# Attention and two gated layers on one core: buffers as fixed tiles, maxima on 64 rows, reciprocals by a DRAM row, another order

## The chip, the cores and the metric

The kernel runs on one core of a Trainium2 chip. The metric is the device time of one execution, in microseconds (us). Engines are named as the profile names them: PE (TensorE, matmuls), PEld (its loads of weights, which overlap it), DVE (VectorE), ACT (ScalarE), POOL (GpSimd), SP (SyncE, which here only issues DMAs).

## What is computed

Attention for 4 batches of 8 heads, 576 positions of 64 numbers each, with a mask of blocks of 64; its result, 4 x 576 x 512, goes through a gated layer with a convolution, and that one's result through a second layer, gated along the positions. Cut to what matters, the reference is:

```python
def _attn_ref(q, k, v):                      # 4, 8, 576, 64
    scores = scale * np.matmul(q, k.transpose(0, 1, 3, 2))
    scores = np.where(block_i >= block_j, scores, -1e9)
    scores = scores - np.max(scores, axis=-1, keepdims=True)
    attn = np.exp(scores)
    attn = attn / (np.sum(attn, axis=-1, keepdims=True) + 1e-09)
    return np.matmul(attn, v)

def _moe_ref(x, w_in, conv_w, w_out):        # 512 -> 1024 -> 512
    h = np.maximum(x @ w_in, 0.0)
    conv_out = sum(conv_w[k] * shift(h, k - 1) for k in range(3))
    return (h * sigmoid(conv_out)) @ w_out

def _moe2_ref(x, w_in, w_spatial, b_spatial, w_out):
    h = np.maximum(x @ w_in, 0.0)
    u, v = h[..., :512], h[..., 512:]
    v_n = (v - mean(v)) / np.sqrt(var(v) + 1e-06)
    v_s = np.einsum('ts,bsd->btd', w_spatial, v_n) + b_spatial[None, :, None]
    return (u * v_s) @ w_out
```

## The kernel before

**Numbers in two parts.** TensorE multiplies values that are rounded to a shorter format in one pass, full float32 in four. To keep accuracy, most operands are held as a rounded value and a low part (`_h`, `_l`), and a product is three products: high by high, low by high, high by low. Making the two parts (a rounding copy and a subtraction, `minus`, `sub` L331) is work of ACT, POOL and DVE.

**Pairs.** Attention works on 16 pairs of heads, counted here from 0; four pairs make a batch. One pair passes through these steps:

- `prep_pair` (L461 to L508) loads q and k of a pair (`raw`, two heads on 128 partitions) and rounds them into `kp` and `qbd`. `qbd` is block-diagonal: nine blocks of 128 x 128, in which head 0's 64 queries stand on partitions and columns 0 to 63, head 1's on 64 to 127, and the rest is zero. Pairs 0 to 5 (`PF32` = 6) multiply their scores in float32 from `raw`; later ones also make low parts `kl`.
- `max_step` (L521) finds the maximum of each query over the keys it may see. Ten products with the 128 rows of `qbd`: for block 0 to 7 over 64, 128, ... 512 keys, for the last block two of 288. VectorE reduces each with its own TENSOR_REDUCE (L544; L537 for the last block in one). `max_tr` (L557) transposes the 128 x 9 maxima on TensorE (L563), copies them to `mt`, and a DMA for each head (L576) writes them as a row behind the queries, `mq`.
- `score`, `unit` (L604 to L664): products of keys and queries of the two heads abreast, each on 64 of the 128 rows (L620 in float32, L628 in parts), and one that adds mask and maximum (`mk`, `mq`, L632). ScalarE takes the exponentials (L641).
- `av` (L666): the attention values (L325), and with them the sums: for pairs 0 to 6 (`PONES` = 7) all as products with ones; for the others `add_up` (L695) adds the exponentials on DVE or POOL first.
- `v_out`, `s_out`, `norm_a`, `norm_b` (L713 to L782): values to `xpair`, sums to `srow`. A DMA (L742) packs the sums into `rc`, 36 x 32; DVE takes the reciprocal (L746); it is split into `rh` and `rl`, two DMAs (L756) write both as rows of `r4`, and TensorE spreads them over the partitions with a selector matrix `sel` (float32 rounded, 4 products with sums on PE, else 2; L761). DVE multiplies `xpair` by this from PSUM (L772); POOL rounds the result to `x` (L328), DVE or POOL makes its low part (L331).

**Dense layers.** `in1` (L788) makes one chunk of the hidden layer, 12 products of 290 columns; ACT, DVE (L814, two taps), ACT, DVE (L819) and POOL (L328) turn it into `g`. `out1` (L833) multiplies `g` by `w1o`, 24 products of 288 columns a chunk, in two parts. The weights come as 64-bit numbers in 512 KB pieces and are put together by `split64` (L402) and `words_to_f32` (L386): ACT, three on DVE (L394, L396, L398), a rounding on ACT and a subtraction. What follows attention (the second layer: `vtile`, `ustep`, `sstep`, `ostep`) works on one batch at a time.

**What sets the order.** Nothing in the program runs in a loop of its own: an `Order` object plays the kernel through in advance, with a cost for each step, and so fixes the sequence of instructions on every engine. Each step is a generator that takes a place in a ring of buffers, waits for marks, and queues work for an engine. TensorE's next step is chosen by `pick_at` from five streams: maxima (`xstream`, released by `next_x` with `XE` and `XK`), scores, values, `norm_b`, and the dense layers (`mstream`); `AHEAD` says how far each batch's dense layers may run ahead of attention. A change between products on 64 rows and on 128 rows has a cost there (`tile`). All loads are issued by SP in one sequence; the costs of a DMA are in `dma`. Buffers are rotating pools (`tag`, `bufs`): the next allocation takes the buffer that is the next in turn.

```python
MSTEPS = [[(0, 0, 0, 0, 64), (0, 64, 1, 0, 128), (0, 192, 2, 0, 192), (1, 0, 3, 0, 256)],
          [(0, 0, 4, 0, 320), (1, 0, 5, 0, 384)], [(0, 0, 6, 0, 448), (1, 0, 7, 0, 512)],
          [(0, 0, 8, 0, HT), (1, 0, 8, HT, HT)]]
```

Of the kernel before, what the change touches and what calls it, by code (L numbers as in the profile page):

```python
# [16 lines left out]
NP = H // 2  # L17
# [12 lines left out]
AHEAD = (0.47, 0.62, 0.22, 0.75)  # L30
PREP_AT = 8
PREP_DT = 2.5
PREP_DT2 = 2.5
PREP_AT2 = 36
# [3 lines left out]
PF32 = 6  # L38
X1KEEP = (0, 1)
PONES = 7  # L40
KL_POOL = 0xbe22
QL_POOL = 0xaa37
SGN_POOL = 0x1
M_ACT = 0xd8c6
Q_DVE = 0x0
PTWO = 5
P_KL = 2
NPR = 0
SPLIT = 2
# [40 lines left out]
class Order:  # L90
# [9 lines left out]
    def __init__(self, rings):  # L100
# [18 lines left out]
        self.times = {r: [-9.0] * n for r, n in rings.items()}  # L119

# [8 lines left out]
    def advance(self, gen, group):  # L129
        while True:  # L130
            try:
                it = next(gen)
            except StopIteration:
                self.live[group] -= 1
                return
            kind = it[0]
            if kind == "mark":
                self.mark(it[1])
            elif kind == "free":
                self.release(it[1], it[2] if len(it) > 2 else 1)  # L140
# [83 lines left out]
    def pe(self):  # L224
# [5 lines left out]
        for r, n in step["rings"]:  # L230
            self.grab(r, n)
# [3 lines left out]
        after = step["fn"]()  # L235
# [48 lines left out]
def attn_moe_moe2_kernel(  # L284
# [19 lines left out]
        "raw": NRAW, "mq": NQ, "kpq": NKP, "v": 2, "e0": NE[0], "e1": NE[1], "es": NES, "late": NRAW - 1, "xp": 2, "sr": 1, "r4": 1,  # L304
# [150 lines left out]
    def prep_pair(p, t):  # L455
# [35 lines left out]
        if p < PF32:  # L491
            return
# [972 lines left out]
```

## Time and profile before

| | |
|---|---|
| median of 3 runs | 604.42 us (603.97 to 608.26) |
| profiled execution | 608.3 us, span from first to last instruction 606.5 us |
| PE busy | 586.5 us (97%) |
| PEld busy | 526.9 us (87%) |
| DVE busy | 453.2 us (75%) |
| ACT busy | 258.6 us (43%) |
| POOL busy | 187.4 us (31%) |

The table by stretch in the rows below has one line for each piece of the span: from and to, its length, then for PE, PEld, DVE, ACT and POOL the busy us with the number of instructions, the clock granted to TensorE (1.00 is full), the busy share of the DMA engines and their GB/s. A line of a timeline gives start and length in us, the engine, the line of the program, output and inputs, the shape, and how often in a row; in brackets is how long it waited and for whom. Matmuls overlap, so a printed length is longer than the distance to the next start; prices of products are distances between starts. A line by form gives count, busy us and mean ns of one, and the idle time of the engine just before.

### The profile page before, as it was taken

To read this page: it belongs to the slowest core of one execution; us is meant where nothing else is said; L and a number is where in the kernel's file an instruction comes from. 1 tells how busy PE (TensorE), PEld (TensorE's weight loads), DVE (VectorE), ACT (ScalarE), POOL (GpSimd) and SP (SyncE) were. 2 spreads that over 40 slices of the span, in tenths; PEclk is the share of its full clock that TensorE was granted. 3 is DMA by queue.
4 is the path that set the end of the run, shared out by engine and by line. 5 is a ranking of instruction groups with operands and counts; after the bars stand their busy time and mean duration, and the time that the engine had idled before them with its cause. 6 is when DMAs were issued, how large, how long until landed. Compare 5 with 4: busy or idle time off the path is not lost.

```text
span 606.5 us, 12028 instructions
## 1 busy us (share of the span) xinstructions
PE 586.5 (97%) x4654; PEld 526.9 (87%) x4654; DVE 453.2 (75%) x964; ACT 258.6 (43%) x528; POOL 187.4 (31%) x237
## 2 busy tenths in 40 slices
PE   7989999999999999999999999999999999999997
PEld 5656679798888888989988999888989999998997
DVE  6889999886786985786938398977894676368257
ACT  4666645635436733526624375545342023013101
POOL 7323213533444353344503144442221112022021
PEclk9899999999999999999999999999999999999999
DMA  7555530214014014021010555335603300610012
GB/s 246 166 173 172 197 105 31 83 41 141 23 61 121 24 41 144 21 65 39 21 60 2 161 179 180 108 108 163 227 0 112 123 21 2 195 40 2 13 48 78
DMA packets 41927, 56.65 MB, mean 93 GB/s; under 512 B 9381, under 2 KB 34725, under 8 KB 41870
## 3 DMA queue, kind: packets, MB, share of 16 engines
q1 hardware_dynamic: 41380, 55.72, 28.7%
q8 instruction: 36, 0.59, 0.4%
q0 software_dynamic: 400, 0.16, 0.1%
q14 instruction: 21, 0.17, 0.1%
q10 hardware_dynamic: 90, 0.01, 0.0%
HBM read 41.42 MB, written 14.16 MB: 92 GB/s over the span
## 4 chain that ended last, share of the span: by engine, by line
PE 62%; DVE 23%; DMA 5%; POOL 3%; issue 2%; ACT 2%; SPq 1%; DVEq 0%; POOLq 0%; ACTq 0%
PE mo L317 38%; PE st L317 13%; PE st L325 4%; DVE cc L814 4%; PE st L628 4%; DVE mx L544 3%; DMA w_raw<-in_w2i_dram 2%; DVE w_f L398 2%; DVE w_raw L396 2%; DMA w_raw<-in_w1i_dram 2%; PE st L632 2%; PE st L620 2%; DVE cc L819 1%; DVE w_raw L394 1%; DVE g L331 1%
## 5 line engine op out<-in xcount | busy, mean ns | idle before, releaser
L317 PE MATMUL mo<-g,w1o_h 128*128 128x288 f32 x496 | 105.3, 298 | 1.2 <-DVE y L852 1.2
L317 PE MATMUL mo<-x,w1i_h 128*128 128x290 f32 x488 | 105.3, 301 | 0.7 <-ACT h L807 0.6
L317 PEld LDWEIGHTS mo<-g,w1o_h 128*128 128x128 f32 x496 | 81.5, 189 | 3.2 <-DVE y L852 1.6
L317 PEld LDWEIGHTS mo<-x,w1i_h 128*128 128x128 f32 x488 | 80.7, 189 | 3.3 <-ACT h L807 1.6
L814 DVE SCALAR_TENSOR_TENSOR cc<-h,cwt,cc 128x288 f32<-128x288 f32 x128 | 72.9, 583 | 10.2 <-ACT cc L811 9.6
L328 POOL TENSOR_SCALAR g<-cc 128x288 fp32r<-128x288 f32 x64 | 39.8, 624 | 113.4 <-DVE cc L819 108.2
L317 PE MATMUL mo<-g,w1o_l 128*128 128x288 f32 x248 | 73.2, 295 | 0.0
L317 PE MATMUL mo<-x,w1i_l 128*128 128x290 f32 x244 | 72.4, 297 | 0.0
L641 ACT ACTIVATE e<-st 128x640 f32<-128x640 f32 (+1 forms) x64 | 52.3, 837 | 29.7 <-PE st L632 29.0
L328 POOL TENSOR_SCALAR gt<-ga 128x288 fp32r<-128x288 f32 x40 | 19.8, 496 | 113.9 <-DVE ga L1160 74.1
L317 PE MATMUL mo<-x,w2i_h 128*128 128x288 f32 x256 | 52.2, 296 | 1.5 <-ACT u L1135 1.5
L544 DVE TENSOR_REDUCE mx<-st 128x1 f32<-128x320 f32 (+7 forms) x98 | 43.9, 481 | 5.6 <-PE st L317 5.3
L317 PEld LDWEIGHTS mo<-g,w1o_l 128*128 128x128 f32 x248 | 46.6, 188 | 0.2
L325 PE MATMUL st<-e,v 128*64 128x448 f32 (+4 forms) x384 | 46.7, 392 | 0.0
L317 PEld LDWEIGHTS mo<-x,w1i_l 128*128 128x128 f32 x244 | 46.1, 189 | 0.1
L325 PEld LDWEIGHTS st<-e,v 128*64 128x64 f32 x384 | 25.0, 137 | 23.4 <-issue 16.5
L317 PEld LDWEIGHTS mo<-x,w2i_h 128*128 128x128 f32 x256 | 41.4, 188 | 2.3 <-ACT u L1135 2.0
L317 PE MATMUL mo<-ws_h,vnh 128*128 128x288 f32 x135 | 39.3, 295 | 1.1 <-issue 1.1
L632 PE MATMUL st<-mq,mk 64*128 64x320 f32 (+1 forms) x192 | 37.7, 385 | 1.9 <-DMA mq<-mt 1.9
L317 PE MATMUL st<-w2i_h,x 128*128 128x512 f32 x128 | 39.5, 390 | 0.0
L331 DVE TENSOR_TENSOR gt<-ga,gt 128x288 fp32r<-128x288 f32 x56 | 25.5, 476 | 17.5 <-POOL gt L328 17.5
L811 ACT ACTIVATE cc<-h,cwt 128x288 f32<-128x288 f32 x64 | 34.1, 538 | 10.2 <-POOL g L335 6.0
(171 smaller groups left out, 1427.3 us busy)
## 6 DMA issues: line engine op xcount, KB each, us to landing
x2d<-y SPq DMA_DIRECT2D x32, 288.0 KB
x<-x2d SPq DMA_DIRECT2D x16, 576.0 KB
raw<-in_kq_dram SPq DMA_DIRECT2D x15, 576.0 KB
v<-in_vt_dram SPq DMA_DIRECT2D x16, 320.0 KB
out_dram<-o SPq DMA_DIRECT2D x32, 144.0 KB
w_raw<-in_w1i_dram SPq DMA_DIRECT2D x8, 512.0 KB
w_raw<-in_w1o_dram SPq DMA_DIRECT2D x8, 512.0 KB
w_raw<-in_w2i_dram SPq DMA_DIRECT2D x8, 512.0 KB
```

Of the source, the lines that this page charges most:

```text
L317: nc.tensor.matmul(o, w, x, start=start, stop=stop)
L325: nc.tensor.matmul(o[row:row + m], w, x, start=start, stop=stop)
L328: nc.gpsimd.tensor_scalar(o, i, 1.0, 0.0, ALU.mult, ALU.add)
L331: nc.vector.tensor_tensor(o, a, b, ALU.subtract)
L396: yield ("DVE", t_dve(n), lambda: nc.vector.scalar_tensor_tensor(r[:, :, 1], r[:, :, 0], 29, r[:, :, 1], ALU.logical_shift_right, ALU.bitw ...
L398: yield ("DVE", t_dve(n), lambda: nc.vector.scalar_tensor_tensor(f.bitcast(U32), f.bitcast(U32), 3, r[:, :, 1], ALU.logical_shift_left, AL ...
L544: yield ("DVE", t_dve(n), lambda: nc.vector.tensor_reduce(mx[:, c:c + 1], st[bk][:, o:o + n], AX.X, ALU.max), 0, 0)
L628: nc.tensor.matmul(st[:, e, o:o + nq], keys(kx, slice(64 * e, 64 * e + 64)), qx[e], start=j == 0, stop=False)
L632: nc.tensor.matmul(st[:, e, o:o + nq], keys(mk, r), q[r, q0:q0 + nq], start=False, stop=True)
L641: yield ("ACT", t_act(2 * n), lambda: nc.scalar.activation(ex[:, :, e0:e0 + n], st[:, :, 0:n], ACTF.Exp, scale=0.125), 0, 0)
L811: yield ("ACT", t_act(HT, False, 1), lambda: nc.scalar.activation(cc, h[:, o:o + HT], ACTF.Copy, scale=cwt[:, c, 1:2]), 0, P_G)
L814: yield ("DVE", t_dve(HT, ptr=1), lambda: nc.vector.scalar_tensor_tensor(cc, h[:, o + e:o + e + HT], cwt[:, c, j:j + 1], cc, ALU.mult, ALU ...
```

## The change

**Fixed tiles.** `Order` gets `slots`: `grab` returns the buffers themselves, in the order in which they came free, and `release` gives them back. Instead of pools that rotate there are fixed tiles, and whichever comes free first is the next.

**Maxima on 64 rows.** `qbd` goes. The rounded queries `qp` have the form of `kp`, two heads on 128 partitions, and only the last block stands block-diagonally in `qlast`. For the first 512 queries, `tile_max` multiplies 128 queries of one head by their keys on 64 rows, both heads one after the other into the two banks of a buffer: 128, 256, 384 and 512 columns. Since of 128 queries the upper 64 see 64 keys more, VectorE reduces in two instructions (all 128 partitions without the last 64 keys, and the upper 64 partitions over these), and `max_up` combines. `last_max` has the two products of 288 columns. These products count as `tile` steps now, as the scores do.

**Reciprocals by DRAM.** `rh`, `rl`, `r4`, `sel`, the selector products and the step `norm_b` go. The reciprocals `rc` are written to a row in DRAM, `rd`, and two DMAs read each head's row into 64 partitions of `rb` (`broadcast_to`). DVE multiplies `xpair` by `rb`, in one piece for pairs without sums on PE, and in three for the others.

**Numbers of the order.** Most of the planner's numbers and of the masks that say which engine does which copy change. Pairs with float32 scores are now 0, 1, 2, 4, 6, 7 and 9 (`F32_PAIRS`). A DMA's cost in the plan is changed (`RATE`, `HEAD`, `SLACK`).

```diff
-AHEAD = (0.47, 0.62, 0.22, 0.75)
-PREP_AT = 8
-PREP_DT = 2.5
-PREP_DT2 = 2.5
-PREP_AT2 = 36
+AHEAD = (0.05, 2.01, -0.09, 0.71)
+PREP_AT = 5.0
+PREP_DT = 1.4
+PREP_DT2 = 4.05
+PREP_AT2 = 45.0
-PF32 = 6
+F32_PAIRS = 0x2d7
-MARGIN = 0.4
+MARGIN = 0
-ADD_DVE = 0xffca
+ADD_DVE = 0x3674
-XE = (0.5, 1.75)
-XMO = 7
+XE = (0.95, 13.95)
+XMO = 11
...
     def grab(self, ring, n):
         self.free[ring] -= n
         del self.times[ring][:n]
+        got = self.slots[ring][:n]
+        del self.slots[ring][:n]
+        return got
...
-    yield ("DMA", size / 360e3 + 0.01, None, 0, 0)
-    yield ("sleep", DMA_LAG)
+    yield ("DMA", size / RATE + 0.01, None, 0, 0)
+    yield ("sleep", DMA_LAG + (SLACK if size > 65536 else 0.0))
...
+    QTILES = [[(0, 0), (1, 128)], [(2, 0)], [(3, 0)]]
+    def tile_max(p, j, i):
+        def fn(got):
+            kp, qp, _ = KPQ[p]
+            mx, up = maxima(p)
+            st = got["st"][0]
+            for c, o in QTILES[i]:
+                n = 128 * c + 128
+                for e in range(2):
+                    r = slice(64 * e, 64 * e + 64)
+                    nc.tensor.matmul(st[:, e, o:o + n], qp[r, 128 * c:128 * c + 128], kp[r, 0:n], start=True, stop=True)
...
+                for c, o in QTILES[i]:
+                    yield red(mx[:, c:8:4], st[:, :, o:o + 128 * c + 64])
+                if i == 0:
+                    yield red(up[64:128].rearrange("p (e c) -> p e c", e=2)[:, :, 0:2],
+                              st.rearrange("p e (i x) -> p e i x", x=256)[64:128, :, :, 64:128])
+                else:
+                    c = i + 1
+                    yield red(up[64:128, c:8:4], st[64:128, :, 128 * c + 64:128 * c + 128])
...
+    def last_max(p, j, ring):
...
+            for i in range(2):
+                mm(st[i][:, 0:HT], ql8, kp[:, HT * i:HT * i + HT], True, True)
...
+    def max_up(p):
+        for j in range(4):
+            yield ("wait", ("mx", p, j))
+        mx, up = MX[p]
+        yield ("DVE", 0.08, lambda: nc.vector.tensor_tensor(mx[64:128, 0:8], mx[64:128, 0:8], up[64:128], ALU.max), 0, 0, True)
...
     def norm_a(p, sr):
...
         yield ("DVE", 0.26, lambda: nc.vector.reciprocal(rc, rc), 0, NPR)
-        if (M_ACT >> p) & 1:
-            yield ("ACT", 0.2, lambda: nc.scalar.activation(rh, rc, ACTF.Copy), 0, NPR)
-        else:
-            yield ("DVE", 0.12, lambda: nc.vector.tensor_copy(rh, rc), 0, NPR, True)
-        yield ("DVE", 0.13, lambda: sub(rl, rc, raw(rh)), 0, NPR, True)
-        yield ("take", "r4")
-        def rows():
-            for t, x in enumerate((rh, rl)):
-                nc.sync.dma_start(out=raw(r4[2 * t:2 * t + 2, :]), in_=raw(x))
-        yield from dma(9216, rows, 0, 1.35)
+        yield from dma(4608, lambda: nc.sync.dma_start(out=rd[p], in_=rc), 0, 0.66)
         yield ("free", "rc")
+        yield ("take", "rb")
+        rb = att.tile([128, S], F32, name="rb", tag="rb", bufs=1)
+        def spread():
+            for e in range(2):
+                nc.sync.dma_start(out=rb[64 * e:64 * e + 64], in_=rd[p][e:e + 1].broadcast_to([64, S]))
+        yield from dma(294912, spread, 0, 0.9)
+        yield ("wait", ("vo", p))
+        cols = [(0, S, 0)] if not pe_sums(p) else [(0, 160, 0), (160, 448, 128), (448, S, -HT)]
+        for lo, hi, o in cols:
+            yield ("DVE", t_dve(hi - lo), lambda: nc.vector.tensor_tensor(
+                x[:, lo:hi], x[:, lo:hi], rb[:, lo + o:hi + o], ALU.mult), 0, NPR, True)
```

Three places show what this does to the instructions. The first is TensorE behind the transposition of pair 1's maxima (L563 before, L647 after), where pair 2's maxima and pair 0's attention values follow. Before:

```order
L563 MATMUL st<-ident,mx 9x128
L317 MATMUL mo<-kp,qbd_97 128x64
L317 MATMUL mo<-kp,qbd_97 128x128
L317 MATMUL mo<-kp,qbd_97 128x192
L317 MATMUL mo<-kp,qbd_97 128x256
L317 MATMUL st<-kp,qbd_97 128x320
L317 MATMUL st<-kp,qbd_97 128x384
L317 MATMUL st<-kp,qbd_97 128x448
L317 MATMUL st<-kp,qbd_97 128x512
L325 MATMUL st<-e_167,v 64x128 x2
```

After (`qp` are the rounded queries, `qlast` the last block; x2 are the two heads):

```order
L647 MATMUL st_111<-ident,mx 9x128
L342 MATMUL mo_108<-kp_153,qlast_150 128x288
L342 MATMUL mo_109<-kp_153,qlast_150 128x288
L587 MATMUL st_110<-kp_153,qp_154 128x128 x2
L587 MATMUL st_110<-kp_153,qp_154 128x256 x2
L587 MATMUL st_111<-kp_153,qp_154 128x384 x2
L350 MATMUL st_112<-e_127,v_125 64x128 x2
```

Eight products of 128 rows have become two of 128 rows (the last block, which stood apart before) and three pairs of 64 rows; the pair of 512 columns comes after the next score step.

The second place is the SP queue around the reciprocals of pair 0. Before:

```order
L742 DMA rc<-srow 36x1x32
L413 DMA w_raw<-in_w1i_dram 128x4x256
L461 DMA raw<-in_kq_dram 128x1152
L413 DMA w_raw<-in_w1i_dram 128x4x256
L756 DMA r_99<-rh 2x18x32
L756 DMA r_99<-rl 2x18x32
L576 DMA mq_96<-mt 1x9x64
L413 DMA w_raw<-in_w1i_dram 128x4x256
```

After (`rd` is the row in DRAM, `rb` the spread reciprocals, `x` places that hold raw weights):

```order
L828 DMA rc<-srow 36x1x32
L455 DMA x_434<-in_w1i_dram 128x4x256
L831 DMA rd_59<-rc 36x32
L502 DMA raw<-in_kq_dram 128x1152
L660 DMA mq_148<-mt_139 2x4x128
L660 DMA mq_148<-mt_139 2x1x64
L838 DMA rb<-rd_59 64x576 x2
L455 DMA w_raw_141<-in_w1i_dram 128x4x256
```

The two small rows `r` have become a row to DRAM and two reads of it, with a load of q and k and the rows of maxima in between; a pair's maxima are now written by two DMAs, one of 2 x 4 x 128 and one of 2 x 1 x 64.

The third place is VectorE up to the last reduction of pair 6's maxima. Before (L394, L396, L398 put the weights together, L331 makes the low part of `w1o`, L551 combines the last block):

```order
L396 SCALAR_TENSOR_TENSOR w_raw<-w_raw 128x512
L394 TENSOR_SCALAR w_raw<-w_raw 128x512
L398 SCALAR_TENSOR_TENSOR w_f<-w_f,w_raw 128x512
L396 SCALAR_TENSOR_TENSOR w_raw<-w_raw 128x512
L398 SCALAR_TENSOR_TENSOR w_f<-w_f,w_raw 128x512
L733 TENSOR_SCALAR srow<-st 128x288
L331 TENSOR_TENSOR w1o_l<-w_f,w1o_h 128x512
L544 TENSOR_REDUCE mx<-mo 128x1
L331 TENSOR_TENSOR w1o_l<-w_f,w1o_h 128x512
L772 TENSOR_TENSOR xpair<-xpair,st 128x576
L544 TENSOR_REDUCE mx<-mo 128x1
L551 TENSOR_TENSOR mx<-mx 128x1
```

After (L439, L441, L443 are the same steps for the weights, L844 multiplies by `rb`, L640 is `max_up`):

```order
L830 RECIPROCAL rc<-rc 36x32
L844 TENSOR_TENSOR xp_130<-xp_130,rb 128x288
L439 TENSOR_SCALAR w_raw_141<-w_raw_141 128x512
L439 TENSOR_SCALAR x_847<-x_847 128x512
L844 TENSOR_TENSOR xp_130<-xp_130,rb 128x128
L441 SCALAR_TENSOR_TENSOR w_raw_141<-w_raw_141 128x512
L441 SCALAR_TENSOR_TENSOR x_847<-x_847 128x512
L592 TENSOR_REDUCE mx<-st_112 128x2
L513 CAST qp_154<-raw 128x576
L592 TENSOR_REDUCE mxu<-st_112 64x2
L443 SCALAR_TENSOR_TENSOR w_f_137<-w_f_137,w_raw_141 128x512
L640 TENSOR_TENSOR mx<-mx,mxu 64x8
```

Two low parts of `w1o` stood here and five in all up to this point; after, one is done by here, and two more pieces of weights are under way.

## Rows read from the trace of the kernel before

**Rows 1.** Page, part 1: busy us, share of the span and instructions.

```profile
PE 586.5 (97%) x4654; PEld 526.9 (87%) x4654; DVE 453.2 (75%) x964; ACT 258.6 (43%) x528; POOL 187.4 (31%) x237
```

**Rows 2.** By stretch (us): length, busy us of each engine, granted clock, DMA share, GB/s.

```profile
45.00:82.00 37.00, 34.88 (x369) 24.38 (x365) 35.76 (x80) 25.12 (x41) 9.71 (x10) 0.98 0.58 188
82.00:144.00 62.00, 60.18 (x566) 52.96 (x566) 52.16 (x105) 29.09 (x61) 23.37 (x27) 1.00 0.17 53
144.00:349.00 205.00, 204.18 (x1726) 184.48 (x1724) 150.88 (x305) 97.03 (x201) 73.43 (x84) 1.00 0.21 66
```

**Rows 3.** Timeline of TensorE: start, length (us), engine, line, operation; in brackets its wait.

```profile
82.16 0.27 PE L563 MATMUL st<-ident,mx 128*9 128x128 f32 x1 [0.88 <-DVE mx L551]
82.36 0.81 PE L620 MATMUL st<-raw 64*128 64x320 f32 x4
83.15 0.49 PE L620 MATMUL st<-raw 64*128 64x192 f32 x4
...
143.97 0.27 PE L563 MATMUL st<-ident,mx 128*9 128x128 f32 x1
```

**Rows 4.** Timeline of TensorE: maxima (qbd), selector (sel) and their neighbours.

```profile
67.26 0.56 PE L317 MATMUL st<-r,sel 128*128 128x160 f32 x4
67.74 0.70 PE L620 MATMUL st<-raw 64*128 64x256 f32 x4
...
149.97 0.93 PE L317 MATMUL st<-kp,qbd 128*128 128x64 f32 x6
150.74 0.29 PE L317 MATMUL mo<-x,w1i_h 128*128 128x290 f32 x1
...
153.95 0.60 PE L317 MATMUL st<-kp,qbd 128*128 128x448 f32 x2
154.48 1.94 PE L325 MATMUL st<-e,v 128*64 128x128 f32 x12
```

**Rows 5.** Timeline of TensorE: score products of two heads, each row a pair.

```profile
144.48 0.36 PE L628 MATMUL st<-qbd,kl 64*128 64x448 f32 x2
144.68 0.37 PE L628 MATMUL st<-kl,kp 64*128 64x448 f32 x2
...
145.24 0.28 PE L628 MATMUL st<-kl,kp 64*128 64x64 f32 x2
145.35 0.28 PE L632 MATMUL st<-mq,mk 64*128 64x64 f32 x2
145.46 0.39 PE L628 MATMUL st<-qbd,kp 64*128 64x320 f32 x2
...
146.13 0.25 PE L628 MATMUL st<-qbd,kp 64*128 64x192 f32 x2
```

**Rows 6.** By line and form, reductions of maxima on VectorE: busy us, mean ns.

```profile
L537 DVE TENSOR_REDUCE mx<-st 128x1 f32<-128x576 f32 x10 | 7.5, 752 | 2.8 <-PE st L317 2.8
L544 DVE TENSOR_REDUCE mx<-st 128x1 f32<-128x64 f32 x9 | 1.9, 214 | 0.2 <-PE st L317 0.2
```

**Rows 7.** By line and form: hidden layer's taps, and x of a pair on VectorE, GpSimd.

```profile
L814 DVE SCALAR_TENSOR_TENSOR cc<-h,cwt,cc 128x288 f32<-128x288 f32 x128 | 72.9, 583 | 10.2 <-ACT cc L811 9.6
L772 DVE TENSOR_TENSOR xpair<-xpair,st 128x576 f32<-128x576 f32 x16 | 11.9, 746 | 1.0 <-PE st L317 1.0
L331 DVE TENSOR_TENSOR x<-xpair,x 128x576 fp32r<-128x576 f32 x11 | 9.3, 846 | 1.9 <-POOL x L328 1.9
L328 POOL TENSOR_SCALAR x<-xpair 128x576 fp32r<-128x576 f32 x16 | 14.3, 892 | 42.3 <-DVE xpair L772 36.2 <-issue 4.1 <-ACT cc L811 1.8
```

**Rows 8.** Timeline: two small transfers, from the SP queue's issue to whoever waits.

```profile
10.93 0.95 SPq L576 DMA_DIRECT2D mq<-mt  x1
...
14.38 0.72 PE L632 MATMUL st<-mq,mk 64*128 64x320 f32 x2 [0.40 <-DMA mq<-mt]
...
117.70 0.63 SPq L742 DMA_DIRECT2D rc<-srow  x1
...
119.47 0.34 DVE L746 RECIPROCAL rc<-rc 36x32 f32<-36x32 f32 x1 [0.20 <-DMA rc<-srow]
```

More of the change, by code (lines that the diff above doesn't have):

```diff
@@ L234, in pe @@
         self.tile = tile
-        after = step["fn"]()
+        after = step["fn"](got)
         self.pe_free = self.t + self.cost
@@ new lines, in max_done, with maxima, task, red @@
+    def max_done(p, j):
+        return lambda: [("kpq", [KPQ[p]])] if j == 3 and f32_scores(p) else []
+    def maxima(p):
+        if p not in MX:
+            MX[p] = (att.tile([128, NBLK], F32, name="mx", tag="mx", bufs=2), att.tile([128, 8], F32, name="mxu", tag="mxu", bufs=2))
+        return MX[p]
+    def tile_max(p, j, i):
[6 more added lines that the diff above has]
+                for e in range(2):
+                    r = slice(64 * e, 64 * e + 64)
+                    nc.tensor.matmul(st[:, e, o:o + n], qp[r, 128 * c:128 * c + 128], kp[r, 0:n], start=True, stop=True)
+                od.cost += max(n / 2400 + 0.015, 0.105)
+            def task():
+                def red(o, i):
+                    return ("DVE", t_dve(2 * i.shape[-1] * (i.shape[2] if len(i.shape) == 4 else 1)), lambda: nc.vector.tensor_reduce(o, i, AX.X, ALU.max), 0, 0)
+                for c, o in QTILES[i]:
[6 more added lines that the diff above has]
+                    yield red(up[64:128, c:8:4], st[64:128, :, 128 * c + 64:128 * c + 128])
+                yield ("free", "st", st)
+                yield ("mark", ("mx", p, j))
+            return [(task(), "att")]
+        return dict(needs=[("kpq", p, i, x) for i in range(2 if p == 0 and j else 1) for x in range(2)], rings=[("st", 1)], fn=fn,
+                    frees=max_done(p, j), tile=True)
@@ L829, in in1 @@
         first = dict(alts=ALTS, base=[("g", 1)]) if ks[0] == 0 else dict(rings=[])
-        d = dict(first, needs=[("x", NP * b + k) for k in ks] + [("w1i", c)], fn=fn, w=0.37 * len(ks), frees=[("x1", 4)] if last else [])
+        d = dict(first, needs=[("x", NP * b + k) for k in ks] + [("w1i", c)], fn=fn, w=0.37 * len(ks),
+                 frees=lambda: [("x1", [X1N.pop(NP * b + k) for k in range(KD)])] if last else [])
         return d
@@ L1013, in attn_moe_moe2_kernel @@
     od.spawn(prep_all_w1(), "w1")
[L1014 removed]
+    od.run(lambda: pos["v"] == len(vstream) and od.over("att"))
     p1.close()
[L1016 to L1020 removed]
+    ps_s2 = ctx.enter_context(tc.tile_pool(name="ps_s2", bufs=1, space=PS))
+    slots("st", ps_s2, 6, [128, 512], F32, "s2")
     od.extra["st"] = 0
```

606 lines of the change are left out of this document (300 added, 306 removed).

## The prediction

> **What bounds the kernel now.** I read the busy line first [rows 1]: TensorE is busy for 586.5 of 606.5 us, VectorE for 453.2. A share over the whole span hides stages, so the table by stretch comes next [rows 2]. I cut it at two events that both kernels have: the transposition of the maxima of pair 6 (82.16 us) and that of pair 9 (143.97 us) [rows 3]; pairs are counted from 0. From 0 to 82 us VectorE is the bound. From 45 to 82 us it is busy 35.76 of 37.00 us, and the row at 82.16 shows TensorE standing still for 0.88 us until VectorE has combined maxima. From 82 us on TensorE is the bound: 60.18 of 62.00 us, then 204.18 of 205.00 us, while VectorE idles for 9.8 and 54 us. So what a cheaper product is worth depends on where it stands: nothing before 82 us, its full price behind that.
>
> Two prices recur. One matmul of the dense stages takes 0.134 us: between the rows at 150.74 and 153.95 us [rows 4] stand 24 of the hidden layer. VectorE's instructions overlap a little: printed durations times counts add up to 506 us over all its groups, the page says 453.2 for 964 instructions [rows 1], so I count each at its duration minus 0.055 us.
>
> **The change, part by part.**
>
> *Maxima on TensorE.* Before, six products (64 to 384 columns) take 150.74 - 149.97 = 0.77 us, those of 448 and 512 columns 0.53 us with the step into the next row shape (0.43 without), the two of 288 columns 2 x 0.134 = 0.27 [rows 4]: 1.47 us for a pair. After, 128, 256, 384 and 512 columns run for two heads at once. The score products already have this form: two of 448 columns start 0.20 us after the two before them, two of 64 columns 0.11 us [rows 5]; 448 columns of one matmul alone are about as long, by the 0.134 us that 290 take. So two heads cost as much as one. At those rates: 0.11 + 0.12 + 0.17 + 0.23 + 0.27 (the 288s stay) = 0.90 us. That is 0.57 us less for each of 16 pairs, 9.1 us. If the two heads did not overlap it would be 1.53 us and a small loss.
>
> *Selector products.* 7 pairs lose four products (67.74 - 67.26 = 0.48 us [rows 4]), 9 lose two (0.27 us): 5.8 us. Steps between row shapes go from 76 to 72, about nothing. One more pair scores in f32: for 320 columns 0.79 us (82.36 to 83.15 [rows 3]) against 0.67 us (145.46 to 146.13 [rows 5]), over 1600 columns up to 0.6 us more. I take TensorE's total as 14.5 us less; bounds 8 (f32 and steps at their worst, overlap only partly won) and 15.5.
>
> *VectorE.* The reductions change shape. A reduction costs 0.148 us plus 1.05 ns an element (0.214 us at 64, 0.752 us at 576 [rows 6]). Before, a pair has eight of 64 to 512 elements, together 3.57 us, plus the last block. After, it has 128, 384, 640 and 896 elements (two heads in one), three extra on 64 partitions (256, 128, 128) and one combining: 4.0 us. With 0.055 us off each, that is about +0.4 us a pair. Splitting the reciprocal (one or two small instructions a pair) goes. The multiplication by the reciprocals was 0.746 us with one operand in PSUM; after, both lie in SBUF, in one piece for 9 pairs and three for 7. No row shows it. The bounds are that 0.746 us and the 0.846 us of a subtraction of the same size with both operands in SBUF [rows 7], 1.6 us over all pairs; I take the lower, 0.9 us for three pieces. The sums of five of nine pairs move to GpSimd, all of them from pair 7 on, where VectorE has room. Over the span VectorE does about 14 us less. Before pair 6's maxima it does not: counted row by row in the two orders, 69.2 us of work stand there before and 68.0 us after (maxima +4.0; weights -5.6, as nine of their instructions come later; the two memsets of the old operand -1.7; casts +1.4; the rest +0.7).
>
> *The new order.* The postponed weights come back. Between the transpositions of pairs 6 and 9 VectorE has 50.2 us in the new order: maxima 12.8, hidden layer 16.7 and its low parts 3.0, weights 9.1, the rest 8.6. TensorE has 58.2 us there before (61.8 on the clock, so 1.06 times the rows' prices) and 47.4 after: 36 second-layer products and one attention-value group of the shorter kind (about 3.4 us) now stand behind pair 9. Maxima run up to three pairs ahead and hold the PSUM buffers until VectorE has reduced them.
>
> *Reciprocals through DRAM.* One small transfer becomes two in a row, the second 295 KB in two issues. A small landing takes from 1.8 us (117.70 to 119.47) to 3.4 us (10.93 to 14.38, with loads in flight) [rows 8]. So x of a pair comes 2 to 5 us later. What hides it: in the new order 96 second-layer products (12.9 us) stand between the last pair's values and the first product that needs its x, and the path (copy and multiplication at 0.75 each, three landings of 1.8 to 2.5, reciprocal 0.34, rounding 0.89, low part 0.85 [rows 7, 8]) is 9 to 11 us. I cost it at nothing; without that cover it would be 3 us, once or twice. *Fixed tiles* take away waits for a buffer out of turn; behind 82 us TensorE idles 8 us in all, so 0 to 2 us, taken as 0.
>
> **The sum**, against the profiled execution (span 606.5 us, run 608.3):
> - To pair 6's transposition: 82.2 us were 69.2 of VectorE's work and 13.0 of its idle time, most of it at the start. With 68.0: 81.0 us.
> - From there to pair 9: TensorE 47.4 x 1.06 = 50.3, VectorE 50.2. Two equal streams don't mesh fully; with 2 us: 52 us, was 61.8.
> - Behind pair 9: 462.5 us before; TensorE's rows add up to 444.4 before and 448.7 after, so 466.8.
>
> Together 599.8 us of span, 6.7 less. TensorE gives up 14.5 us, but what it saves ahead of pair 6 is lost behind VectorE. From the median of 604.4 that makes 597.7; I say 597.5.
>
> The Trainium skill, TensorEngine Tiling, Performance Considerations (PSUM Bottleneck), says tiling speeds up TensorE but not the emptying of PSUM, which may become the bottleneck. This trace agrees up to 82 us and speaks against it behind that, where VectorE idles. By that rule alone the change would bring nothing.
>
> **The rivals.**
> - *VectorE keeps its idle time between pairs 6 and 9.* It idled there 9.8 us before; the hidden layer's taps alone wait 9.6 us for ScalarE over the span [rows 7]. If a stream that is now the bound still waits so, the stretch takes 60 us and the span is 607.8: median 605.5, no change. For it: a hidden-layer chunk passes from ScalarE to VectorE, back, again to VectorE, to GpSimd and often back. Against: while TensorE was the bound such idling was free, and from 45 to 82 us VectorE idled 1.2 us only. Half of it gives 601.5.
> - *The front shrinks too.* Much of the 13.0 us is start-up; loads are spaced anew. If 5 us of it goes and the streams mesh, 14 us are won: 590.5. Against: the first load, first maxima and first row transfer stay in series.
> - *Slower: the SP queue.* It issues in order; the copy of a pair's reciprocals waits for their landing in DRAM, and rows of maxima and loads queue behind it. If the order expects 1.8 us and the landing takes 3.4, SP stands 1.6 us, 16 times. From 0.8 us a pair reaching TensorE (12.8 us) the kernel is 6 us slower: 610.5. For it: the 3.4 us row [rows 8]. Against: in the order other transfers stand between write and copy, so most of the landing passes anyway.
> - The Trainium skill, DMA: Bandwidth & Descriptors, gives about 2.0 us of fixed cost for a DMA; it lies between this trace's 1.8 and 3.4, and by it alone that rival would not come up.
> - *The heads don't overlap* in the maxima: 0.06 us a pair lost, 607 from the median. The score rows speak against it; under 3 in 100.
>
> **How the numbers follow.** The forecast (594 to 600.5) has 0.47, the first rival 0.27, the shrinking front 0.14, SP 0.10, no overlap 0.02. The likeliest case gives 597.5. The range 588 to 606 takes in the first three and their halves, and leaves out SP and the far end of the front. One per cent is 6 us, about what a measurement of this kernel can tell from no change. Below 598.4 lie the front and most of the forecast: 0.56 faster. The rest of the forecast and the first rival make 0.35 within 1%. SP at its worst: 0.09 slower.
>
> **What would show it.** Right: pair 6 transposed at 80 to 82 us and pair 9 at 131 to 135; the maxima's pairs of 512 columns 0.23 us apart; VectorE near full from 45 to 130 us; TensorE dense behind. Wrong: pair 9 at 140 or later (first rival); pair 6 at 76 or earlier (front); long SP waits at the copy of the reciprocals, with score products waiting for rows of maxima; gaps of TensorE ahead of a batch's first hidden-layer product (x too late).

## The result and the profile after

The changed kernel takes 612.75 us (median of 17 runs, 610.9 to 615.53), the kernel before 606.36 us (17 runs, 603.97 to 610.62): 1.0103 times as long, 95% interval 1.0083 to 1.0122. I had forecast 597.5 us and a range of 588 to 606. The change made the kernel slower by 1%, and the prediction is wrong in sign and in size.

Engines of the changed kernel, in the order of [rows 1] (page, part 1):

```profile
PE 582.1 (95%) x4596; PEld 519.1 (85%) x4596; DVE 458.7 (75%) x930; ACT 252.8 (41%) x517; POOL 220.3 (36%) x269
```

TensorE lost 4.4 us of busy time (7.0 in the second profile below) where I expected 14.5; VectorE gained 5.5 where I expected it to lose 14. The three stretches of my sum, cut at the transpositions of pairs 6 and 9, first in this profile (an execution of 615.53 us, the longest of the 17), then in a second one of the same kernel (612.32 us, near the median); columns as in [rows 2]:

```profile
0.00:86.62 86.62, 68.61 (x656) 48.57 (x656) 70.14 (x156) 43.93 (x76) 29.85 (x39) 0.86 0.52 171
86.62:142.29 55.67, 52.56 (x449) 44.02 (x449) 51.32 (x103) 31.24 (x64) 26.30 (x27) 0.94 0.27 94
142.29:613.80 471.51, 460.98 (x3493) 426.50 (x3491) 337.28 (x672) 177.66 (x379) 164.10 (x203) 1.00 0.28 87
```

```profile
0.00:81.60 81.60, 65.41 (x656) 45.55 (x656) 70.18 (x155) 43.85 (x76) 30.44 (x39) 0.91 0.57 182
81.60:139.05 57.45, 53.24 (x449) 45.20 (x449) 51.32 (x103) 31.30 (x64) 26.17 (x27) 0.92 0.28 91
139.05:610.50 471.45, 460.89 (x3495) 426.48 (x3491) 337.30 (x672) 177.83 (x379) 164.23 (x203) 1.00 0.28 87
```

| stretch, us | before | forecast | first profile | second profile |
|---|---|---|---|---|
| to pair 6's transposition | 82.2 | 81.0 | 86.6 | 81.6 |
| from there to pair 9's | 61.8 | 52 | 55.7 | 57.45 |
| behind pair 9's | 462.5 | 466.8 | 471.5 | 471.45 |
| span | 606.5 | 599.8 | 613.8 | 610.5 |

All three come out above the forecast. The granted clock (third column from the end) is 0.86 and 0.91 in the first stretch. Cut by that, TensorE works three times at half its clock, 1.2 instead of 2.4 GHz:

```profile
8.50:26.00 17.50, 11.78 (x50) 7.52 (x52) 12.37 (x27) 8.21 (x16) 3.92 (x7) 0.52 0.40 135
57.40:63.40 6.00, 6.00 (x47) 5.37 (x45) 3.80 (x10) 3.71 (x7) 0.00 (x0) 0.50 0.26 85
88.00:94.40 6.40, 6.40 (x37) 5.54 (x39) 6.32 (x15) 3.99 (x7) 1.69 (x2) 0.50 0.62 234
```

That is 30 us; the kernel before had 10 (12.5 to 18.8 and 43 to 46.4 us). Ahead of each stretch TensorE waits. Of the second one, some rows in order of time (TensorE, VectorE, ScalarE; those between are left out):

```profile
54.10 0.40 PE L587 MATMUL st<-kp,qp 64*128 64x512 f32 x2
55.69 0.46 DVE L819 TENSOR_SCALAR srow<-st 128x288 f32<-128x288 f32 x1
56.24 0.65 ACT L805 ACTIVATE xp<-st 128x576 f32<-128x576 f32 x1 [0.59 <-DVE srow L819]
56.95 0.58 PE L712 MATMUL st<-qp,kp 64*128 64x256 f32 x2 [2.45 <-ACT xp L805]
57.97 0.57 PE L712 MATMUL st<-qp,kp 64*128 64x448 f32 x2
58.34 0.57 PE L712 MATMUL st<-qp,raw 64*128 64x448 f32 x2
62.31 0.38 PE L647 MATMUL st<-ident,mx 128*9 128x128 f32 x1
62.73 0.28 DVE L654 CAST mt<-st 9x128 fp32r<-9x128 f32 x1 [2.09 <-PE st L647]
```

The three PSUM buffers hold maxima, scores and a pair's values with their sums. The sums leave at 55.69, since VectorE is at weights and at the low part of another pair's x until then, the values at 56.24 behind them, and TensorE stands for 2.45 us until that buffer is free. Behind that, two products of 448 columns start 0.37 us apart instead of 0.20 [rows 5], until 63.4. Now VectorE, so far the bound, waits 2.09 us for TensorE.

### The profile page after: what moved, and what is told of

It reads as the page before. It is cut to its first block, busy times and chain, and to the rows that moved or that the text cites. A ratio compares the mean times of both kernels' runs of the same rounds, so it can differ in the third digit from the quotient of the medians.

```text
span 613.8 us, 11943 instructions
## 1 busy us (share of the span) xinstructions
PE 582.1 (95%) x4596; PEld 519.1 (85%) x4596; DVE 458.7 (75%) x930; ACT 252.8 (41%) x517; POOL 220.3 (36%) x269
## 4 chain that ended last, share of the span: by engine, by line
PE 56%; DVE 27%; DMA 5%; ACT 4%; issue 3%; POOL 2%; SPq 1%; ACTq 0%; DVEq 0%; POOLq 0%
PE mo L342 33%; PE s L342 9%; DVE cc L882 5%; PE st L350 4%; PE st L712 4%; DVE cc L886 3%; DVE mx L592 3%; PE st L704 2%; DMA w_raw<-in_w2o_dram 2%; DMA raw<-in_kq_dram 2%; PE st L716 2%; DVE g L356 2%; DVE w_f L443 2%; PE st L587 1%; DVE w_raw L441 1%
## 5 line engine op out<-in xcount | busy, mean ns | idle before, releaser
L342 PE MATMUL mo<-x,w1i_h 128*128 128x290 f32 x504 | 109.1, 303 | 1.7 <-DVE y L919 1.2
L342 PE MATMUL mo<-g,w1o_h 128*128 128x288 f32 x464 | 98.3, 298 | 0.8 <-ACT h L876 0.4
L882 DVE SCALAR_TENSOR_TENSOR cc<-h,cwt,cc 128x288 f32<-128x288 f32 x128 | 77.8, 623 | 18.1 <-ACT cc L879 17.5
L342 PEld LDWEIGHTS mo<-g,w1o_h 128*128 128x128 f32 x464 | 76.2, 189 | 3.2 <-issue 1.5
L342 PE MATMUL mo<-g,w1o_l 128*128 128x288 f32 x232 | 68.5, 295 | 0.0
L353 POOL TENSOR_SCALAR g<-ga 128x288 fp32r<-128x288 f32 x40 | 19.0, 474 | 108.3 <-DVE ga L1225 73.4
L342 PE MATMUL mo<-x,w2i_h 128*128 128x288 f32 x256 | 52.4, 296 | 0.5 <-ACT u L1199 0.3
L592 DVE TENSOR_REDUCE mx<-st 128x2 f32<-128x128 f32 (+3 forms) x64 | 42.3, 684 | 4.9 <-PE st L587 3.4
L342 PEld LDWEIGHTS mo<-g,w1o_l 128*128 128x128 f32 x232 | 43.6, 188 | 0.1
L342 PE MATMUL s<-w2i_h,x 128*128 128x512 f32 x128 | 39.5, 390 | 0.0
L884 ACT ACTIVATE cc<-cc 128x288 f32<-128x288 f32 x64 | 28.1, 440 | 27.1 <-DVE cc L882 26.6
```

Source lines behind the costliest of these rows:

```text
L342: nc.tensor.matmul(o, w, x, start=start, stop=stop)
L353: nc.gpsimd.tensor_scalar(o, i, 1.0, 0.0, ALU.mult, ALU.add)
L592: return ("DVE", t_dve(2 * i.shape[-1] * (i.shape[2] if len(i.shape) == 4 else 1)), lambda: nc.vector.tensor_reduce(o, i, AX.X, ALU.max), ...
L882: yield ("DVE", t_dve(HT, ptr=1), lambda: nc.vector.scalar_tensor_tensor(cc, h[:, o + e:o + e + HT], cwt[:, c, j:j + 1], cc, ALU.mult, ALU ...
L884: yield ("ACT", t_act(HT, False), lambda: nc.scalar.activation(cc, cc, ACTF.Tanh, scale=0.5), 0, P_G)
```

## The experiments

Theories: **clock** (half clock is the loss), **VectorE** (its work sets the pace over more of the span than I assumed), **order** (the new numbers are the loss), **steps** (the row in DRAM, or the sums on GpSimd). The table gives the stretches of each profile that leaves the order of instructions as the change has it; VectorE's busy time is in brackets.

| kernel | median, us | to pair 6 | 6 to 9 | behind 9 |
|---|---|---|---|---|
| changed, second profile | 612.75 | 81.6 (70.2) | 57.45 (51.3) | 471.45 (337.3) |
| a1_fill | 611.91 | 80.2 (67.5) | 55.6 (51.3) | 470.8 (337.1) |
| a2_fillgaps | 611.15 | 83.4 (70.5) | 55.6 (49.5) | 470.6 (337.3) |
| a4_noupper | 596.6 | 76.2 (60.4) | 54.4 (45.3) | 467.6 (328.1) |
| a5_peprobe | 616.79 | 84.6 (70.4) | 61.3 (52.3) | 470.5 (337.0) |
| a6_super | 600.54 | 79.1 (63.5) | 53.1 (47.0) | 468.8 (331.2) |
| a7_superearly | 599.05 | 76.2 (64.2) | 52.9 (45.1) | 467.9 (331.0) |
| a8_nosums | 613.04 | 85.6 (70.5) | 55.8 (51.3) | 471.5 (333.4) |
| a10_superfill | 602.14 | 79.9 (62.6) | 52.4 (46.0) | 468.2 (331.2) |

**a1_fill and a2_fillgaps: unread matmuls in TensorE's gaps.** The added matmul is the same in both; a1 places it where the plan is idle, a2 by a list of measured waits.

```diff
         step = self.pick()
         if step is None:
+            self.fill()      # a1: as many as the plan's idle time holds
             return
...
+            nc.tensor.matmul(free[-1][:, 300:512], mk[:, 0:128], mk[:, 0:212], start=True, stop=True)
```

> The changed kernel with its order as it is, and 87 matmuls more whose result nobody reads (128 x 212 columns of a constant into columns of PSUM that nothing else uses), put on TensorE where the ordering program expects it to have nothing to do, up to 100 us. Clock theory: in the changed kernel TensorE stands at half clock (0.50 granted) from 8.5 to 26, from 57.4 to 63.6 and from 88 to 94 us, 30 us in all against 10 us before, each time after a stretch with gaps; work done there takes twice as long, and this is most of the loss. Then the extra matmuls take away part of the half-clock stretches (not all, since the plan sees 8.7 us of idle time and the trace 18) and the kernel takes 605 to 610 us, with the mean granted clock above 0.98. Rival (the gaps are themselves the loss: buffers and VectorE are late, the clock only goes with it): no change, 611 to 614.

> The changed kernel with its order as it is, and 169 such unread matmuls put ahead of those 16 instructions on TensorE that waited 0.25 us or more in the changed kernel's trace up to 100 us, 0.1 us of them for each 0.1 us of wait. Clock theory: the three half-clock stretches go or shrink to below 10 us together, pair 6 is transposed at 82 to 84 us instead of 86.6, pair 9 at 135 to 138 instead of 142.3, and the kernel takes 603 to 607 us. Rival (gaps are the loss, the clock is a companion): the clock rises but pair 6 stays at 86 us, and the kernel at 611 to 614.

a1 took 608.42 to 618.42 us in four runs, 1.0113 times the kernel before (1.0035 to 1.0191), a2 608.75 to 612.39 in ten, 1.0068 times (1.0044 to 1.0091), against 1.0103 of the change. a1's profiled execution, the shortest of its four, has no half-clock stretch:

```profile
0.00:80.20 80.20, 72.65 (x743) 53.13 (x743) 67.47 (x156) 43.95 (x76) 30.77 (x39) 1.00 0.59 185
80.20:135.80 55.60, 50.03 (x452) 41.61 (x450) 51.25 (x103) 31.08 (x64) 26.20 (x27) 1.00 0.29 94
135.80:606.60 470.80, 460.47 (x3493) 426.33 (x3491) 337.09 (x672) 178.13 (x379) 163.88 (x203) 1.00 0.28 87
```

At full clock pair 6 is transposed at 80.2, close to my 81.0, and its span is 4 to 7 us below the two profiles of the change. But the medians gain only 0.8 us (some 3 without a1's slowest run) and 1.6 us, and a1's runs scatter over 10 us. a2's ten runs have a granted clock of 0.995 to 0.998 over the span, those of the change 0.970 to 0.986, and still take 611.15 us; both medians lie in the rival's range, 611 to 614, though a2 brings pair 6 to 83.4 us as the clock theory has it. So the clock is a part, and by these runs the smaller one: it goes with the difference between an execution that reaches pair 6 at 86.6 and one that does at 81.6, and doesn't close the distance to the forecast. The unread matmuls can hold up other work themselves (a2's TensorE is busy for 80.1 of its first 83.4 us), so these gains are a lower bound of what the clock costs.

**a3_oldnum, b1_newnum and b2_dram: other orders.** The first two swap the numbers between the kernels; the third puts the row in DRAM into the kernel before.

```diff
-AHEAD = (0.05, 2.01, -0.09, 0.71)
+AHEAD = (0.47, 0.62, 0.22, 0.75)    # a3: and all others but RATE, HEAD, SLACK; b1: the reverse
```

```diff
-                mm(st[:, j, ...], sel, r4[...], True, True)    # norm_b; rh, rl and r4 go with it
+        yield from dma(4608, lambda: nc.sync.dma_start(out=rd[p], in_=rc), 0, 0.66)
+        yield from dma(294912, spread, 0, 0.9)
```

> The changed kernel's steps (fixed tiles, maxima on 64 rows, reciprocals by DRAM) under the order's numbers of the kernel before (all but the three costs of a DMA, which stay). If the new numbers and the order that follows from them are what costs, this takes 598 to 604 us, my forecast for the steps alone. If the steps themselves cost (the row in DRAM, buffers held by maxima, the clock), it takes 610 us or more, with half-clock stretches as long as those of the changed kernel.

> The kernel before, its steps unchanged, under the new numbers of the order as far as it has them. If the new numbers cost, it takes 610 to 618 us. If the steps cost, it stays at 603 to 608.

> The kernel before with one part of the change: the reciprocals by a row in DRAM instead of the selector products (its numbers as they were, the order follows). My forecast's pricing: the selector products take 6.4 us of TensorE, 4.3 of them behind pair 6 where TensorE is the bound; nothing waits for x, so 601 to 604 us. Rival (x comes late and the SP queue stands): 607 to 612.

625.27, 645.15 and 631.35 us: 19, 39 and 25 us above the kernel before; b1 and b2 lie above all that I had expected of them. a3 alone would say that the steps cost, b1 alone that the numbers cost; both together say that each set of numbers is slow with the other kernel's steps, and the two theories are not told apart. b2 shows how. Waits by engine, TensorE and VectorE of b2:

```profile
PE mo L317 <- ACT h L791: 6.3, 6, 3.4
PE st L317 <- DVE mt L570: 5.2, 2, 4.8
DVE rc L743 <- DMA rc<-srow: 13.9, 6, 5.4
```

In the order that follows, VectorE's reciprocal stands up to 5.4 us ahead of its transfer, everything behind it on VectorE with it, and TensorE waits 4.8 us for a copy of maxima. So b2 says little about the price of the row itself: a part tried under a new order measures the order with it. From here on the order stays as it is, and single instructions are left out, widened or added.

**a4_noupper: without the extra reductions.** The plan keeps their time and issues nothing.

```diff
-                    yield red(up[64:128, c:8:4], st[64:128, :, 128 * c + 64:128 * c + 128])
+                    yield red(up[64:128, c:8:4], st[64:128, :, 128 * c + 64:128 * c + 128], True)   # True: not issued
-        yield ("DVE", 0.08, lambda: nc.vector.tensor_tensor(mx[64:128, 0:8], mx[64:128, 0:8], up[64:128], ALU.max), 0, 0, True)
+        yield ("DVE", 0.08, None, 0, 0, True)
```

> The changed kernel with its order as it is, but without the three reductions of the upper 64 partitions and without the combining instruction of each pair (the maxima then lack 64 keys for half of the queries). That takes 4 instructions and some 1.2 us from VectorE for each of 16 pairs, 11 us of it up to pair 9. If VectorE is the bound up to pair 9's transposition (my forecast's step, 52 us between the pairs 6 and 9 by VectorE), pair 9 comes at 132 to 135 us instead of 142.3 and the kernel takes 602 to 606 us. If buffers and the clock bind, pair 9 comes at 138 or later and the kernel stays above 608.

596.6 us, 0.9833 times the kernel before (0.9798 to 0.9868). 16 us go, more than the 7 to 11 expected, pair 9 comes at 130.6, and 3.85 us of the gain lie behind pair 9, where I had called TensorE the bound.

**a5_peprobe: more TensorE work between pairs 6 and 9.**

```diff
+            for _ in range(6):
+                nc.tensor.matmul(ps[:, 300:512], mk[:, 0:128], mk[:, 0:212], start=True, stop=True)
```

> The changed kernel with its order as it is and 78 unread matmuls of 212 columns, six behind each group of the dense layers between the transpositions of pairs 6 and 9, about 8 us of TensorE. If VectorE is the bound there, most of it vanishes in waits: 612 to 615 us. If TensorE is the bound there (at half clock or not), it costs its whole time: 618 to 621.

616.79 us, 4 us more than the change, for 8.7 us of matmuls. Between the two expectations:

```profile
84.60:145.90 61.30, 60.02 (x528) 52.62 (x528) 52.30 (x103) 31.20 (x64) 25.94 (x27) 0.95 0.27 85
```

Neither engine alone is the bound in that stretch: against the second profile, 8.7 us more on TensorE cost 3.9 there, and 6 us less on VectorE (a4) gave 3. The sizes are rough, since the two profiles of the changed kernel differ by 1.8 us in this stretch: against the first it is 5.6 and 1.3.

**c1_again: a second profile.**

> The changed kernel once more, for a second profile. Clock theory: the length of the half-clock stretches differs from one execution to the next and the time with it; in an execution of 611 to 612 us there are 20 to 25 us at half clock instead of 30. Rival: the stretches are as long (28 to 32 us) in any execution, and the time varies for another reason.

612.32 us, with 24 us at half clock instead of 30 (8.5 to 22.6, 80.6 to 87 and 128.5 to 132 us): as the clock theory has it, the stretches differ between these two executions, and the longer time goes with the longer stretches.

**a6_super, a7_superearly and a10_superfill: fewer reductions.** One reduction takes in all keys of the product for both halves; those of the upper half and the combining instruction go, as in a4.

```diff
-                    yield red(mx[:, c:8:4], st[:, :, o:o + 128 * c + 64])
+                    yield ("DVE", t_dve(2 * (128 * c + 64)), lambda: nc.vector.tensor_reduce(
+                        mx[:, c:8:4], st[:, :, o:o + 128 * c + 128], AX.X, ALU.max), 0, 0)
```

> The changed kernel with its order as it is, but each pair's maxima of 128 queries reduced in one instruction over all their 128 columns more or less: the upper and the lower 64 queries both over all keys of the product, so for the lower 64 the 64 masked keys count too. The value subtracted ahead of the exponential is then the maximum or a little more, which cancels in the quotient. Three reductions and the combining instruction of a pair go, four reductions become 128 elements longer (by 0.13 us each from the rows at 128, 384, 640 and 896 elements): 0.7 us of VectorE less for a pair. Leaving out the upper reductions altogether gave 16 us for 20.2 us of printed time. Theory (VectorE's work on the maxima sets the pace up to pair 9 and partly behind it): 11.7 us printed give 8 to 10 us, 603 to 605 us. Rival (that run gained because its maxima came earlier at one place, not by work): 608 or more.

> As a6_super, and 72 unread matmuls ahead of those seven instructions of TensorE that waited in the first 20 us. Clock theory: the first half-clock stretch (8 to 23 or 26 us in two profiles of the changed kernel) goes, and pair 1 is transposed 1 to 2 us earlier; the kernel takes 1 to 3 us less than a6_super. Rival (VectorE is the bound in the front, TensorE's clock there is hidden): the same time within 1 us.

> As a6_super, with 87 unread matmuls where the ordering program expects TensorE idle up to 100 us, as in a1_fill. Clock theory: the clock stays near full and the kernel takes 3 to 6 us less than a6_super, 598 to 602. Rival, by a1_fill's runs (608 to 618 us): no gain in the median and a wider scatter.

600.54 us (0.9878, 0.9830 to 0.9925), 599.05 us (0.9858, 0.9820 to 0.9896) and 602.14 us (0.9909, 0.9876 to 0.9943; 597.81 to 608.62). a6 lowers VectorE's busy time from 458.8 to 441.7 us and gains 12 us, again more than expected, in all three stretches:

```profile
0.00:79.10 79.10, 66.13 (x657) 46.89 (x658) 63.50 (x129) 44.37 (x76) 30.45 (x40) 0.89 0.58 186
79.10:132.20 53.10, 50.05 (x451) 41.78 (x449) 46.96 (x90) 31.02 (x63) 23.16 (x27) 1.00 0.30 101
132.20:601.00 468.80, 461.04 (x3495) 426.47 (x3491) 331.19 (x648) 178.13 (x379) 165.20 (x203) 1.00 0.28 88
```

a7 with matmuls in the first 20 us has a granted clock of 1.00 throughout and is 1.5 us below a6, with intervals that overlap; spread over 100 us (a10) they bring nothing. a6 and a7 are faster than both kernels.

**a8_nosums: without GpSimd's additions.**

```diff
-                yield ("POOL", t_ptt(2 * (S - q0)), lambda: nc.gpsimd.tensor_tensor(o, a, i, ALU.add), 0, P_ADD, True)
+                yield ("POOL", t_ptt(2 * (S - q0)), None if p > 7 else lambda: nc.gpsimd.tensor_tensor(o, a, i, ALU.add), 0, P_ADD, True)
```

> The changed kernel with its order as it is, without GpSimd's additions of the exponentials for pairs 8, 11, 14 and 15 (those sums are wrong then): 16 instructions and some 21 us of GpSimd go. Theory of the port: VectorE's instructions with two operands in SBUF take twice as long while GpSimd's TENSOR_TENSOR runs (taps 0.506 against 1.009 us), 39 us of VectorE's printed time in the changed kernel against 22 before; without the additions VectorE's busy time falls by 8 to 12 us, all of it behind pair 8. As TensorE is the bound there, the kernel gains 1 to 3 us: 609 to 611. Rival (VectorE is a bound there too): 8 us or more, 604 or less. Second rival (no contention): VectorE's busy time stays, 612 to 613.

613.04 us: no gain. VectorE's busy time falls by 3.6 us only, not by 8 to 12, all of it behind pair 9. So the sums of these four pairs on GpSimd are not what makes the change slow.

## Why the prediction was wrong, point by point

Two steps failed. The first is the path: "its full price behind that" made TensorE the bound behind pair 6; my sum gave VectorE a share up to pair 9, with 2 us for the meshing, and counted its work at nothing behind that. With the order fixed, 25.0 us less of VectorE's busy time (a4) made the kernel 16.2 us faster and 17.1 us less (a6) 12.2 us, part of it behind pair 9. The second is the size of two terms: a pair's maxima cost TensorE 0.25 us less and not 0.57, and VectorE's busy time, "about 14 us less", rose by 5.5 us.

**What bounds the kernel.** Right to 82 us, too sharp behind. "Its full price behind that" took TensorE as the bound alone. a4 and a6 changed nothing but VectorE's work and gained 3.85 and 2.65 us behind pair 9. TensorE's busy time there stayed (460.9, 460.5, 461.0); its idle time fell from 10.6 to 7.1 and 7.8. A place where VectorE holds TensorE although it has 134 us of idle time in that stretch (first profile):

```profile
200.45 0.29 DVE L795 TENSOR_TENSOR es<-es,e 64x128 f32<-64x128 f32 x1
200.66 0.16 DVE L640 TENSOR_TENSOR mx<-mx,mxu 64x8 f32<-64x8 f32 x1
200.87 0.28 PE L647 MATMUL st<-ident,mx 128*9 128x128 f32 x1 [1.27 <-DVE mx L640]
```

The last instruction of a pair's maxima stands behind sums and taps, and the transposition waits 1.27 us.

**Maxima on TensorE: the saving was put too high.** I priced a pair at 0.90 us, 0.57 less than before. The rows (timeline of TensorE):

```profile
153.76 0.53 PE L342 MATMUL st<-kp,qlast 128*128 128x288 f32 x2
154.22 0.67 PE L587 MATMUL st<-kp,qp 64*128 64x128 f32 x6
154.82 0.40 PE L342 MATMUL mo<-x,w1i_h 128*128 128x290 f32 x1
...
163.30 0.50 PE L587 MATMUL st<-kp,qp 64*128 64x512 f32 x2
163.63 0.31 PE L712 MATMUL st<-qp,kp 64*128 64x320 f32 x2
```

0.46 + 0.60 + 0.33 = 1.39 us, with the steps between row shapes in it. The two heads do start together, 0.003 us apart, but pairs of 128, 256, 384 and 512 columns cost 0.16, 0.17, 0.26 and 0.31 to 0.34, not 0.11 to 0.23 as score products do. Behind pair 9, 60 maxima products of 6 pairs take 9.66 us of TensorE before and 8.13 after: 0.25 us less for a pair, not 0.57. By its price this is near the rival without overlap (1.53), to which I gave 0.02, though not by its mechanism, since the two heads do start together. Why these pairs take longer than the score's is open.

**Selector products.** Right: TensorE spent 6.4 us on them, forecast 5.8.

**VectorE.** "About 14 us less" became 5.5 us more. The count of instructions was right, their durations were not constant. Lines by form of the changed kernel:

```profile
L592 DVE TENSOR_REDUCE mx<-st 128x2 f32<-128x896 f32 x16 | 17.4, 1088 | 0.9 <-PE st L587 0.8
L592 DVE TENSOR_REDUCE mxu<-st 64x2 f32<-64x128 f32 x32 | 9.4, 296 | 0.6
L592 DVE TENSOR_REDUCE mxu<-st 64x4 f32<-64x256 f32 x16 | 6.8, 424 | 0.1
L640 DVE TENSOR_TENSOR mx<-mx,mxu 64x8 f32<-64x8 f32 x16 | 3.7, 232 | 0.5
L844 DVE TENSOR_TENSOR xp<-xp,rb 128x576 f32<-128x576 f32 x9 | 8.1, 901 | 0.7 <-DMA rb<-rd 0.6
L844 DVE TENSOR_TENSOR xp<-xp,rb 128x160 f32<-128x160 f32 x7 | 4.1, 591 | 0.1
L882 DVE SCALAR_TENSOR_TENSOR cc<-h,cwt,cc 128x288 f32<-128x288 f32 x128 | 77.8, 623 | 18.1 <-ACT cc L879 17.5
```

The reductions are as priced: printed times of all maxima go from 71.8 to 79.2 us, 7.4 more (forecast 6.4). The multiplication by the reciprocals goes from 11.9 to 17.7 us: I took the lower bound (0.746) for one piece and 0.9 for three; it is 0.90 and, with all three pieces, 1.37. The taps and gates of the hidden layer, which the change doesn't touch, go from 108.0 to 115.7 us; 7.2 us of that are instructions that run beside a TENSOR_TENSOR of GpSimd (last section). And the printed durations of all of VectorE's instructions add up to 505.7 us, against 506.4 before: that busy time rose all the same is overlap, 0.050 us an instruction where I had counted 0.055.

**To pair 6.** 81.0 forecast, 81.6 and 86.6 measured, 80.2 at full clock. VectorE's work was right (70.2 us busy against 70.8 before). I had not considered TensorE's clock here at all. It falls after gaps, and gaps there are more than before (18.0 us of idle time up to pair 6 in the first profile, 10.1 before); 2.8 us of them are products of maxima that wait for a reduction of the upper 64 partitions.

**Between pairs 6 and 9.** 52 forecast, 57.45 and 55.7 measured. VectorE is busy 51.3 us (forecast 50.2); the 2 us that I took for two streams that don't mesh are 4.4 to 6.1. That is the mechanism of my first rival, at half its size. Half clock may add to it, but need not: the first profile has 6.4 us of half clock in this stretch and 55.7 us, a1 none and 55.6.

**Behind pair 9.** 466.8 forecast, 471.5 measured: 1.9 us from the price of the maxima, 2.4 us of idle time of TensorE (10.6 against 8.2 us), the rest below half a microsecond.

**Reciprocals by DRAM, SP, fixed tiles.** TensorE never waits for x in the changed kernel's list of waits, and only once (1.2 us, the first pair) for a row of maxima. The cover held, and the rival of the SP queue did not come up. This rests on the waits alone: no run takes the row or the fixed tiles out with the order kept.

Where the forecast's gain went, in one sum over the second profile against the forecast: 0.6 + 5.45 + 4.65 = 10.7 us. On TensorE the maxima saved about 5 us less than priced (16 pairs, 0.32 us each), and what was saved went into waits for VectorE, whose work on the maxima grew by 7.4 us printed. A printed microsecond of maxima on VectorE is worth 0.8 us of the kernel by a4 (16.2 us for 20.9) and 1.1 by a6 (12.2 for 10.9); by this estimate the 7.4 us more come to 6 to 8 us, about the 6.4 us by which the change is slower. a6 takes that growth back (68.3 us printed, below the kernel before): VectorE is then busy for 11.5 us less than before the change, near the 14 that I had forecast, and the kernel takes 600.54 us, about the gain that I had forecast. No run leaves reductions out of the kernel before, so whether VectorE's work weighs as much there is open, and so is what the new numbers of the order cost or give by themselves.

## What to carry to other kernels

An engine that is idle a quarter of the time can still set the pace, if what it does last is what the busiest engine needs next; a leave-out run with the order fixed measures that in one go, a busy share does not. When a cheaper matmul form asks for more reductions, price the reductions first: here 0.25 us of TensorE for a pair were paid with 0.5 us of VectorE. And where a planner's numbers suit one set of steps only, as a3 and b1 suggest, parts can't be tried under a new plan: keep the order and change single instructions.

## What the runs showed of the hardware

VectorE's instructions with two operands in SBUF wait if they begin while GpSimd is at work. Timeline of GpSimd and VectorE in the changed kernel:

```profile
142.37 2.12 POOL L797 TENSOR_TENSOR es<-e,e 128x896 f32<-128x896 f32 x1 [5.07 <-ACT e L725]
142.61 0.28 DVE L654 CAST mt<-st 9x128 fp32r<-9x128 f32 x1 [1.60 <-PE st L647]
142.92 2.19 DVE L356 TENSOR_TENSOR raw<-raw,qp 128x576 fp32r<-128x576 f32 x1
...
228.52 2.12 POOL L797 TENSOR_TENSOR es<-e,e 128x896 f32<-128x896 f32 x1
229.08 0.30 DVE L592 TENSOR_REDUCE mxu<-st 64x2 f32<-64x128 f32 x1
229.41 1.26 DVE L640 TENSOR_TENSOR mx<-mx,mxu 64x8 f32<-64x8 f32 x1
```

A subtraction of 576 elements takes 2.19 us, where alone such take 0.75; a maximum of 8 elements takes 1.26 us instead of 0.16 and ends with GpSimd's addition. A reduction out of PSUM (0.30) and a cast out of PSUM (0.28) in the same time are not slowed.

Over the second profile the taps take 0.506 us alone (45 of them) and 1.009 where more than half of one lies beside a GpSimd TENSOR_TENSOR (18). What decides is who began first. The 16 taps that began while a TENSOR_TENSOR ran took 1.06 us (median), the 30 that began while a TENSOR_SCALAR ran 0.67, the other 82, which began alone or ahead of GpSimd's instruction, 0.51. Of the 46 that came second, 39 ended about 0.3 us after GpSimd's instruction, whichever it was.

Each VectorE instruction's time above the median of its form without a GpSimd TENSOR_TENSOR adds up to 39 us, 22 before. The change moved four additions of each of five pairs to GpSimd and took the multiplication's second operand from PSUM (0.745 us, the same beside GpSimd) to SBUF; both add to this. But a8_nosums, without 16 of the 20 additions, lowers the 39 us by 4.4 only. The rest stands beside GpSimd's other TENSOR_TENSORs, 60 in both kernels, at other places of the order; no run shows what they cost the kernel. The 16 additions cost VectorE time and the kernel none that a8 could show.

The Trainium skill, SBUF — State Buffer, section on SBUF's two separate sides, says that VectorE instructions with two SBUF inputs and GpSimd's share one port pair and that whoever comes second is blocked for the whole instruction. The 2.19 and 1.26 us agree, and so do the taps, those beside a TENSOR_SCALAR too.

TensorE's clock: at 1.2 GHz the same products stand 0.37 us apart instead of 0.20, for 3.5 to 17.5 us after a stretch with gaps, and the stretches differ from one execution to the next of the same program. Unread matmuls in the gaps kept 2.4 GHz throughout in the profiled executions of a1 and a7; the medians gained 0.8 and 1.5 us by it, and nothing in a10.
